# Decay attention and a top-128 expert layer in one kernel: the hand-written planner gets a limit of eight transfers under way, and new places for the operands of heads two and three

## The chip, the cores and the metric

The kernel runs on 1 core of one Trainium2 chip. The metric is device time in microseconds (us) from start to end of one execution; the time given for the kernel before is the median of 3 runs, 458.39 us (456.5 to 458.89). The engines are PE (matrix products and transposes), DVE (vector), ACT (activation), POOL (GpSimd) and SP, which here only issues transfers (DMAs). ACT issues a few DMAs too, at the start.

## The reference

Shapes: q, k, v are (8 batches, 8 heads, 576 rows, 64), f is (8, 8, 576). Everything is float32.

```python
scores = q @ k.T / sqrt(64)
cum = cumsum(log(clip(f, 1e-4, 1)), -1)
scores = where(causal, -1e9, scores + cum[:, None] - cum[None, :])
attn = softmax(scores);  o = attn @ v            # per batch and head
x = o with the heads side by side                # (8, 576, 512)
# per batch:
s = x @ w_gate;  top = the 128 rows with the largest s
h = relu(x[top] @ w1)                            # w1 is (512, 1024)
out = x;  out[top] += sigmoid(s[top]) * (h @ w2) # w2 is (1024, 512)
```

## The kernel before

**Heads and pairs.** The 64 heads are worked two by two, 32 pairs; the pairs of a batch are followed by the batch's expert layer, interleaved with the pairs of the next batch. Matrix products take float32 operands split into a rounded part and a rest. So a head `h` needs four operand tiles: `q2` (rounded q above, its rest below), `kk` (rounded k, twice), `qe` (rounded q and two rows of the decay) and `ke` (the rest of k and two rows of the decay). There are four sets of them, `q2_0` to `q2_3` and so on, used by head `h % 4`. `head_parts(h)` (L410) records what makes them:

- `t_load` (L419) loads q and k of the head into `raw` (two DMAs of 288 KB; three `raw` buffers),
- three casts `a0`, `a1`, `a2` (L448 to L451) make `q2`, `kk`, `qe`. Their line in the profile is L429 on ACT, L431 on DVE, L433 on POOL. For heads below `HELP1` = 16 any of the three engines may take them, later heads use POOL,
- two subtractions `a3`, `a4` (L456, L458; profile line L438) make the rests; DVE does them for heads 0 to 3, POOL for the others,
- the decay rows come by small DMAs: for heads 0 and 1 straight from `ep` in SBUF, issued by ACT (`ext`, profile line L463); for the others from DRAM copies `eq`, `eqr` (stored by ACT at L341, loaded by SP at L475, L478).

**A pair** (`pair_parts`, L492) has nine units, one per 128 rows of a head and one shared. In a unit PE makes scores `sc` (two products: L528 or L564 with `kk`, `q2`; L533 or L564 with `ke`, `qe`), DVE adds the mask and takes the row maximum `nm` (L538, L570, L576), ACT takes the exponential `p` (L589), PE transposes it into `tp` (L602, L620, L622), and ACT or DVE copies that to `pt` (L281, L283). When all nine are copied PE multiplies by v (`av`, L664), the result `ot` is copied and transposed back (`tb`, L717), and DVE normalises it and forms the gate's sums (L723 to L751). PSUM has eight banks, and scores, transposes and `av` all take from these eight.

**The expert layer** (`moe_parts`, L815): DVE counts for each row how many rows have a larger score (`rank`, L893, profile line L901; 14 operations per batch), then the chosen rows are gathered by POOL, transposed, multiplied by w1 and w2 on PE (L1017 to L1078), and scattered by POOL (L1089). The weights come in twelve parts (`weight_part`, L788).

**What sets the order.** Nothing is issued while it is recorded. Each step is handed to `Flow.add` (L58) with its cost in us on each engine that may do it, the steps it comes after, the buffers it takes and gives, and a `place`, a number that ranks it. `Flow.run` (L86) then plays the program on clocks of its own: for each engine it looks at the steps that can start within `EPS` of the earliest, picks the one with the smallest place, advances that engine's clock and issues the step. An engine's queue is in the order in which its steps were picked, and each engine executes its queue in that order. A transfer in the plan takes its time on SP's (or ACT's) clock to issue, 0.63 us for each DMA of a `load`, and its bytes at 240 KB/us on one bus (L113 to L116).

**Places.** `place` is counted in units, nine to a pair. `PS` (L184) sets how far ahead of its use a head's casts stand, `PL` (L183) its load, `PV` (L185) the load of v, `PM`, `PE_`, `PC` the maximum, exponential and copy of a unit, `WS`, `WD`, `WL` the weights, `RK`, `RD` the rank operations, `GO`, `GS`, `GL` the expert layer's products.

Of the kernel before, what the change touches and what calls it, by code (L numbers as in the profile page):

```python
# [30 lines left out]
class Flow:  # L31
# [7 lines left out]

    LAG = {"pe": 0.2, "act": 0.17, "dve": 0.12, "pool": 0.17, "sp": 0.05}  # L40
    OWN = {"pe": 0.0, "act": 0.1, "dve": 0.1, "pool": 0.08, "sp": 0.0}

# [4 lines left out]
    def __init__(self, slots, eps, bias, weight):  # L47
        self.free = {k: [0.0] * n for k, n in slots.items()}
        self.eps = eps
        self.bias = bias  # L50
        self.weight = weight
        self.kind = None
        self.clock = {}
        self.bus = 0.0
        self.ready = []
        self.todo = 0

    def add(self, cost, fn, after=(), place=0.0, take=(), give=(), lat=0.0, kind=None, dma=None):  # L58
        t = {"dma": dma, "cost": cost, "fn": fn, "place": place, "take": take, "give": give, "lat": lat, "kind": kind,
             "wait": 0, "next": [], "deps": [], "end": None, "eng": None, "n": self.todo}  # L60
        for d in after:
            if d is None:
                continue
            t["deps"].append(d)
            d["next"].append(t)
            t["wait"] += 1
        self.todo += 1
        if t["wait"] == 0:
            self.ready.append(t)
        return t  # L70

    def start(self, t, e):
# [4 lines left out]
        for k in t["take"]:  # L77
            n = need.get(k.name, 0)
            f = self.free[k.name]
            if len(f) <= n:  # L80
                return None
            s = max(s, f[n])
            need[k.name] = n + 1
        return max(s, self.clock.get(e, 0.0))

    def run(self, issued):  # L86
        left = self.todo
        while left:
# [24 lines left out]
            if t["dma"] is not None:  # L113

                self.bus = max(self.bus, self.clock[e] + 0.3) + t["dma"]
                t["end"] = self.bus + t["lat"]  # L116
            for k in t["give"]:
                k.end = max(k.end, t["end"] + self.LAG[e])
# [15 lines left out]
def kernel(  # L134
# [33 lines left out]
    BD = 0.35  # L168
    WP = 4
    WQ = 0  # L170
# [7 lines left out]
    LOOK = 6  # L178
    HELP1 = 16
    HELP2 = 4  # L180
    SPLIT = 2
    PR = -10.51
    PL = 19.99  # L183
    PS = 18.31  # L184
    PV = 9.46  # L185
    PM = 0.31
    PE_ = 0.16
    PC = -2.48
    PB = 1.68
    VO = -0.79  # L190
    VD = 1
    GD = 0.1
    WS = 56.75
    WD = 0.5
    WL = 7.32
    RK = 5.98
    RD = 5.85
    XP = 9.4
    GO = 21.21
    GS = 1.93  # L200
    GL = 4.48
    LG = 2.67
    SB = 3
# [87 lines left out]
    def load(fn, kb, n=1, slow=0.0, **kw):  # L291
        return add({"sp": 0.63 * n}, fn, lat=1.2 + slow, dma=kb / 240, **kw)

# [46 lines left out]
    def rows_store(dst, src, us, after, tk):  # L340
        return add({"act": 0.62}, lambda e: nc.scalar.dma_start(out=dst, in_=src().bitcast(F32)), lat=1.3 + us,  # L341
                   after=[after], place=PR, give=[tk])
# [67 lines left out]
    def head_parts(h):  # L410
# [34 lines left out]
        if h < HELP2:  # L445
            c2 = {"pool": 1.46, "dve": 0.9} if h > 3 else {"dve": 0.85}
        pl = base - PS
        a0 = add(c1, rounded(q2[:, cs], lambda: raws[h][:, 0, :]), after=both + old, place=pl)  # L448
# [12 lines left out]
        def ext(dst, src, after, tks, n=0.0):  # L461

            return add({"act": 0.62}, lambda e: nc.scalar.dma_start(out=dst.bitcast(F32), in_=src()), lat=1.3,  # L463
                       after=old + [after], place=h - 40 + n, give=tks)
# [27 lines left out]
    def pair_parts(p):  # L492
# [12 lines left out]

        lv = load(t_v, 288, 2, after=(ops[1][1][-1:] if p == 2 else []) + [d_rows] + avd[p - 3:p - 2] * (p > 2), place=9 * p - PV, take=[tk_v])

# [660 lines left out]
```

## Time and profile before

| | us |
|---|---|
| median of 3 runs | 458.39 |
| the profiled execution | 459.39 |
| its span, first to last instruction | 456.9 |
| PE busy | 430.4 (94% of the span) |
| DVE busy | 371.1 (81%) |
| ACT busy | 331.7 (73%) |
| POOL busy | 302.7 (66%) |

The span is what the rows below speak of; 2.5 us of the profiled execution lie around it. PE is busy for 94% of the span, so idle time of PE is what can be won or added. A row of the timeline gives the start, the duration, the engine, the line in the code, the operation with out<-in, and in brackets how long the engine had been idle before it and what released it. SPq and ACTq are rows of these engines' queues that issue DMAs: the time is that of the issue, not of the transfer.

### The profile page before, as it was taken

What the parts mean: (1) busy time and instruction counts of PE and PEld (TensorE: products, weight loads), DVE (VectorE), ACT (ScalarE), POOL (GpSimd) and SP (SyncE); (2) the same over time, 40 slices, a digit from 0 to 9 for tenths busy, and PEclk for the clock granted to TensorE, in tenths of its full rate; (3) what the DMA queues carried; (4) which work ended last, traced back from release to release, by engine and by line L of the source; (5) the groups of instructions that cost most, each with busy time, mean ns of one, the idle gap of its engine ahead of it and who ended that gap; (6) DMA issues with size and microseconds to landing.
All of it is one profiled execution on the core that took longest, in us unless ns stands there. A gap on an engine that the chain in (4) does not pass through costs nothing. (4 is left out here: it accounts for less than half of the span.)

```text
span 456.9 us, 10456 instructions
## 1 busy us (share of the span) xinstructions
PE 430.4 (94%) x3033; PEld 345.3 (76%) x3033; DVE 371.1 (81%) x1443; ACT 331.7 (73%) x999; POOL 302.7 (66%) x325
## 2 busy tenths in 40 slices
PE   1599999989999999999999999999999999999995
PEld 0588778866787878877877778887887778868773
DVE  7689889997899888999699868897698877885821
ACT  4599989987898787777787778877787678833220
POOL 6379989998899987767766858657667763011100
PEclk9999999998999999999999999999999999999998
DMA  7988869685669787796876586677686551022010
GB/s 189 222 233 231 218 168 248 177 238 156 186 167 241 190 222 188 183 226 165 221 184 180 131 215 160 151 197 182 180 216 159 142 164 45 0 77 76 23 46 24
DMA packets 50514, 75.64 MB, mean 166 GB/s; under 512 B 7863, under 2 KB 35546, under 8 KB 50458
## 3 DMA queue, kind: packets, MB, share of 16 engines
q1 hardware_dynamic: 48790, 70.19, 60.2%
q0 software_dynamic: 1280, 4.20, 2.8%
q10 hardware_dynamic: 388, 0.61, 0.5%
q8 instruction: 24, 0.39, 0.4%
q14 instruction: 32, 0.26, 0.2%
HBM read 56.75 MB, written 12.14 MB: 151 GB/s over the span
## 5 line engine op out<-in xcount | busy, mean ns | idle before, releaser
L589 ACT ACTIVATE p<-p,nm 128x512 f32<-128x512 f32 (+4 forms) x288 | 168.9, 592 | 26.2 <-DVE nm L538 24.3
L538 DVE CUSTOM_DVE_ANT_0 p<-sc,mask 128x384 f32<-128x384 f32 (+3 forms) x256 | 120.0, 484 | 26.9 <-PE sc L533 17.2
L281 ACT COPY pt<-tp 128x256 f32<-128x256 f32 (+3 forms) x246 | 98.5, 436 | 25.3 <-PE tp L602 21.7
L602 PE MATMUL tp<-ident,p 128*128 128x128 f32 x640 | 103.3, 281 | 6.0 <-ACT p L589 5.0
L528 PE MATMUL sc<-kk,q 128*128 128x384 f32 (+3 forms) x256 | 93.1, 368 | 12.5 <-DVE q L438 8.5
L438 POOL TENSOR_TENSOR q<-raw,q 64x576 fp32r<-64x576 f32 x60 | 85.9, 1432 | 12.0 <-DMA xe<-out_dram,idx 7.4
L664 PE MATMUL av<-pt,v 128*64 128x448 f32 (+4 forms) x768 | 93.7, 393 | 0.0
L602 PEld LDWEIGHTS tp<-ident,p 128*128 128x128 f32 x640 | 76.0, 143 | 20.1 <-ACT p L589 7.7
L438 POOL TENSOR_TENSOR ke<-raw,kk 64x576 fp32r<-64x576 f32 x60 | 86.3, 1439 | 4.1
L533 PE MATMUL sc<-ke,qe 68*128 68x384 f32 (+3 forms) x256 | 83.4, 337 | 1.8 <-DMA ke<-ep 1.8
L664 PEld LDWEIGHTS av<-pt,v 128*64 128x64 f32 x768 | 45.7, 137 | 43.5 <-issue 28.6
L433 POOL TENSOR_SCALAR q<-raw 128x576 fp32r<-128x576 f32 x57 | 38.8, 680 | 51.9 <-issue 19.5
L528 PEld LDWEIGHTS sc<-kk,q 128*128 128x128 f32 x256 | 50.2, 197 | 19.7 <-POOL mask L350 8.5
L589 ACT ACTIVATION_READ_ACCUMULATOR p<-p,nm 128x1 f32 x288 | 57.4, 199 | 0.0
L533 PEld LDWEIGHTS sc<-ke,qe 68*128 68x128 f32 x256 | 49.8, 196 | 3.7 <-ACT kk L429 2.2
L281 ACT COPY ot<-av 128x128 f32<-128x128 f32 x64 | 24.6, 398 | 25.7 <-PE av L664 25.5
L901 DVE TENSOR_SCALAR_CACHE_REDUCE j<-srow,sg 128x384 uint8<-128x384 f32 (+6 forms) x72 | 41.4, 575 | 1.2
L1089 POOL DMA_INDIRECT out_dram<-xe,idx x8 | 8.2, 1025 | 51.2 <-DVE xe L1085 49.0
L433 POOL TENSOR_SCALAR kk<-raw 128x576 fp32r<-128x576 f32 x56 | 38.5, 688 | 2.7 <-DMA raw<-in_qk_dram 2.7
L283 DVE COPY pt<-tp 128x128 f32<-128x128 f32 (+2 forms) x74 | 29.2, 401 | 4.6 <-PE tp L602 2.2
L564 PE MATMUL sc<-kk,q 128*128 128x288 f32 x128 | 30.0, 316 | 0.1
L564 PE MATMUL sc<-ke,qe 68*128 68x288 f32 x128 | 28.4, 305 | 0.0
(127 smaller groups left out, 756.8 us busy)
## 6 DMA issues: line engine op xcount, KB each, us to landing
raw<-in_qk_dram SPq DMA_DIRECT2D x128, 288.0 KB
v<-in_v_dram SPq DMA_DIRECT2D x32, 256.0 KB
out_dram<-x SPq DMA_DIRECT2D x16, 512.0 KB
qe<-q SPq DMA_DIRECT2D x41, 144.0 KB
srow<-sd SPq DMA_DIRECT2D x7, 320.0 KB
wst<-in_w_dram SPq DMA_DIRECT2D x4, 512.0 KB
wst<-in_w_dram SPq DMA_DIRECT2D x8, 256.0 KB
v<-in_v_dram SPq DMA_DIRECT2D x32, 32.0 KB
```

The source lines that it names most:

```text
L281: nc.scalar.copy(d, s_)
L283: nc.vector.tensor_copy(d, s_)
L433: nc.gpsimd.tensor_scalar(dst, src(), 1.0, 0.0, ALU.mult, ALU.add)
L438: (nc.vector if e == "dve" else nc.gpsimd).tensor_tensor(dst, a_(), b_, ALU.subtract)
L528: nc.tensor.matmul(st["sc", u][:, :n], q2s[r][:, q_slice(par, i)], kks[r][:, :n], start=True, stop=False)
L533: nc.tensor.matmul(st["sc", u][:, :n], qes[r][0:68, q_slice(par, i)], kes[r][0:68, :n], start=False, stop=True)
L538: nc.vector.tensor_tensor_reduce(out=st["p", u], in0=st["sc", u][:, :n], in1=mask[:, 512 - n:512], scale=-0.125, scalar=BIG, op0=ALU.add, ...
L564: nc.tensor.matmul(st["sc", u][g][:, :HALF], lt[0:kr, sl], rt[0:kr, g * HALF:(g + 1) * HALF], start=(n_ == 0 and m_ == 0), stop=(n_ == 1 a ...
L589: nc.scalar.activation(st["p", u], st["p", u], AF.Exp, bias=st["nm", u], scale=-1.0, accum_out=l)
L602: nc.tensor.transpose(tp[:, pos * P:(pos + 1) * P], st["p", u][:, j * P:(j + 1) * P], ident)
L664: nc.tensor.matmul(avb[g][par * D:(par + 1) * D, q0 - g * SPL:q1 - g * SPL], vt[:, j, par * D:(par + 1) * D], pt[:, off:off + q1 - q0], st ...
L901: nc.vector.tensor_scalar(junk[0:n, 0:w, :], src, sg()[0:n, c:c + 1], None, op, ALU.add, accum_out=cnt[0:n, k, c:c + 1])
```

## The change

`Flow` gets a list `lanes` with the planned end of every DMA in the order in which they are issued, and a constant of 8. A step that issues `k` DMAs can start no earlier than the end of the DMA that stands eight before its last. `load` passes its number of DMAs, the stores and `ext` on ACT pass 1. The casts and rests of heads 2 and 3 (counted from 0) get a place of their own, `P2` = 10 units ahead in place of `PS`. `HELP1` goes from 16 to 13, so casts of heads 13 to 15 are left to POOL; `WP` from 4 to 2, so only the first two weight parts may have their rest on DVE. The v of pair 1, like that of pair 2 before, is not loaded until the decay rows of head 1 are on their way. Twelve other numbers are set anew, most of them by a few hundredths to some tenths of a unit, `PS` from 18.31 to 12.18 and `PV` from 9.46 to 6.15. No operation is added or taken away; some change their engine.

```diff
+    LANES = 8
...
+        n = len(self.lanes) + t["k"] - 1 - self.LANES
+        if t["k"] and n >= 0:
+            s = max(s, self.lanes[n])
         return max(s, self.clock.get(e, 0.0))
...
+            self.lanes += [t["end"]] * t["k"]
...
-    WP = 4
+    WP = 2
...
-    HELP1 = 16
+    HELP1 = 13
     HELP2 = 4
+    P2 = 10
...
-    PS = 18.31
-    PV = 9.46
+    PS = 12.18
+    PV = 6.15
...
     def load(fn, kb, n=1, slow=0.0, **kw):
-        return add({"sp": 0.63 * n}, fn, lat=1.2 + slow, dma=kb / 240, **kw)
+        return add({"sp": 0.63 * n}, fn, lat=1.2 + slow, dma=kb / 240, k=n, **kw)
...
-        pl = base - PS
+        pl = base - (PS if h not in (2, 3) else P2)
...
-        lv = load(t_v, 288, 2, after=(ops[1][1][-1:] if p == 2 else []) + [d_rows] + avd[p - 3:p - 2] * (p > 2), place=9 * p - PV, take=[tk_v])
+        lv = load(t_v, 288, 2, after=(ops[1][1][-1:] if p in (1, 2) else []) + [d_rows] + avd[p - 3:p - 2] * (p > 2), place=9 * p - PV, take=[tk_v])
```

Lines of the new file are 8 higher from `head_parts` on. What the change does to the order shows at three places. The names in the rows carry the set or the unit: `kk_3` is `kk` of head 3, `raw3` its load, `p0_1` the exponential of pair 0, unit 1, `v1` the v of pair 1.

On SP, the queue of loads at the start; before:

```order
L422 DMA raw2_153<-in_qk_dram 64x1152 x2
L499 DMA v0_98<-in_v_dram 128x4x128
L502 DMA v0_98<-in_v_dram 64x128
L499 DMA v1_99<-in_v_dram 128x4x128
L502 DMA v1_99<-in_v_dram 64x128
L422 DMA raw3_196<-in_qk_dram 64x1152 x2
L499 DMA v2_100<-in_v_dram 128x4x128
L502 DMA v2_100<-in_v_dram 64x128
L422 DMA raw4_239<-in_qk_dram 64x1152 x2
```

and with the change:

```order
L430 DMA raw2_153<-in_qk_dram 64x1152 x2
L507 DMA v0_98<-in_v_dram 128x4x128
L510 DMA v0_98<-in_v_dram 64x128
L430 DMA raw3_207<-in_qk_dram 64x1152 x2
L430 DMA raw4_222<-in_qk_dram 64x1152 x2
L507 DMA v1_99<-in_v_dram 128x4x128
L510 DMA v1_99<-in_v_dram 64x128
```

Heads 3 and 4 are loaded ahead of v of pair 1; v of pair 2 has moved down behind the loads of heads 5 to 7.

On ACT, from the end of the `ext` DMAs to the first exponentials; before:

```order
L463 DMA ke_1_109<-ep_163 2x1x576
L429 CAST kk_1_108<-raw1_143 128x576
L429 CAST qe_1_107<-raw1_143 64x576
L341 DMA eq_78<-ep_163 64x1152
L341 DMA eqr_79<-ep_163 128x1x512
L341 DMA eqr_79<-ep_163 128x1x64
L429 CAST q2_2_110<-raw2_153 128x576
L429 CAST kk_2_112<-raw2_153 128x576
L429 CAST qe_2_111<-raw2_153 64x576
L589 ACTIVATE p0_0_180,st0_88<-p0_0_180,nm0_0_212 128x512
L429 CAST kk_3_116<-raw3_196 128x576
L429 CAST qe_3_115<-raw3_196 64x576
```

and with the change:

```order
L437 CAST kk_1_108<-raw1_143 128x576
L437 CAST qe_1_107<-raw1_143 64x576
L437 CAST q2_2_110<-raw2_153 128x576
L437 CAST kk_2_112<-raw2_153 128x576
L471 DMA ke_1_109<-ep_163 2x1x576
L349 DMA eq_78<-ep_163 64x1152
L349 DMA eqr_79<-ep_163 128x1x512
L349 DMA eqr_79<-ep_163 128x1x64
L597 ACTIVATE p0_0_178,st0_88<-p0_0_178,nm0_0_216 128x512
L597 ACTIVATE p0_1_185,st0_88<-p0_1_185,nm0_1_226 128x128
L597 ACTIVATE p0_2_188,st0_88<-p0_2_188,nm0_2_228 128x384
```

The casts of head 3 no longer stand between the first and the second exponential (POOL does them, and `qe_2`); the DMA of the decay rows of `ke_1` has moved behind the casts of head 2.

On DVE, about a fifth of the way through, the first rank operations (`j`); before:

```order
L746 TENSOR_REDUCE gu1_92<-tb5_1509 128x4x2
L901 TENSOR_SCALAR j0_0_1_1592,cnt_97<-srow0_1456,sg0_95 128x640
L901 TENSOR_SCALAR j0_1_0_1613,cnt_97<-srow0_1456,sg0_95 128x128
L901 TENSOR_SCALAR j0_1_1_1617,cnt_97<-srow0_1456,sg0_95 128x512
L901 TENSOR_SCALAR j0_2_0_1637,cnt_97<-srow0_1456,sg0_95 128x256
L901 TENSOR_SCALAR j0_2_1_1648,cnt_97<-srow0_1456,sg0_95 128x384
L751 TENSOR_REDUCE gu1_92<-tb45_1510 64x2
L901 TENSOR_SCALAR j0_3_0_1658,cnt_97<-srow0_1456,sg0_95 128x384
L538 ISA p8_0_1597,nm8_0_1670<-sc8_0_1596,mask_82 128x512
```

and with the change:

```order
L909 TENSOR_SCALAR j0_0_1_1547,cnt_97<-srow0_1419,sg0_95 128x640
L909 TENSOR_SCALAR j0_1_0_1551,cnt_97<-srow0_1419,sg0_95 128x128
L909 TENSOR_SCALAR j0_1_1_1558,cnt_97<-srow0_1419,sg0_95 128x512
L909 TENSOR_SCALAR j0_2_0_1564,cnt_97<-srow0_1419,sg0_95 128x256
L909 TENSOR_SCALAR j0_2_1_1569,cnt_97<-srow0_1419,sg0_95 128x384
L546 ISA p7_7_1519,nm7_7_1577<-sc7_7_1518,mask_82 128x384
L546 ISA nm7_7_1577 128x1
L738 TENSOR_TENSOR x1_0_1368<-tb45_1499,rn1_94 64x128
L746 TENSOR_TENSOR tb5_1498<-tb5_1498,wg_87 128x512
L291 COPY pt7_1427<-tq7_4_1592 128x2x64
L909 TENSOR_SCALAR j0_0_2_1605,cnt_97<-dg0_1553,sg0_95 128x128
L909 TENSOR_SCALAR j0_1_2_1612,cnt_97<-dg0_1553,sg0_95 128x128
```

The same five rank operations stand in one piece in both, but two units earlier with the change, ahead of the work on `tb5` and not near its end.

Over the whole program ACT has 10 casts of heads fewer, DVE 2, and POOL 12 more; ACT has 14 of the `pt` copies and 4 other small ones more, DVE as many fewer. From the middle of the program on, PE's queue is nearly the same in both.

## Rows read from the trace of the kernel before

**Rows 1.** The page's first line, and PE and DVE of its part 1 (busy us, share, instructions).

```profile
span 456.9 us, 10456 instructions
PE 430.4 (94%) x3033; PEld 345.3 (76%) x3033; DVE 371.1 (81%) x1443; ACT 331.7 (73%) x999; POOL 302.7 (66%) x325
```

**Rows 2.** The view of waits, of PE alone: who waited for whom; us in total, times, longest us.

```profile
PE sc L528 <- DVE q L438: 8.5, 1, 8.5
PE tp L602 <- ACT p L589: 5.0, 4, 3.9
PE sc L528 <- DVE nm L538: 2.5, 4, 1.4
PE sc L533 <- DMA ke<-ep: 1.8, 1, 1.8
PE sc L528 <- DVE gu L751: 1.3, 1, 1.3
```

**Rows 3.** Busy time of each engine in stretches of the span: stretch, its length, busy us of PE, of PE's weight loads, DVE, ACT, POOL (in brackets instructions), the granted clock of PE, the DMA engines' share, GB/s.

```profile
16.00:24.00 8.00, 3.75 (x18) 3.42 (x17) 4.89 (x12) 4.25 (x14) 0.68 (x2) 1.00 1.04 240
24.00:40.00 16.00, 16.00 (x112) 14.05 (x111) 14.30 (x52) 15.27 (x47) 14.41 (x13) 1.00 0.92 254
40.00:56.00 16.00, 16.00 (x130) 12.36 (x129) 14.69 (x56) 16.00 (x50) 15.16 (x14) 1.00 0.78 191
56.00:60.00 4.00, 2.72 (x19) 2.03 (x18) 2.27 (x9) 3.56 (x13) 3.08 (x3) 1.00 0.93 261
60.00:96.00 36.00, 35.84 (x286) 28.65 (x285) 33.40 (x119) 34.48 (x108) 34.54 (x33) 1.00 0.76 202
96.00:110.00 14.00, 11.77 (x76) 9.54 (x74) 13.42 (x58) 9.02 (x29) 13.69 (x15) 0.88 0.68 189
...
160.00:430.00 270.00, 269.93 (x1943) 216.65 (x1940) 227.05 (x921) 194.13 (x592) 162.63 (x164) 1.00 0.61 155
```

**Rows 4.** The timeline of PE in the first 25 us.

```profile
11.79 1.51 PE L533 MATMUL sc<-ke,qe 68*128 68x512 f32 x4 [1.80 <-DMA ke<-ep]
...
14.97 0.68 PE L564 MATMUL sc<-ke,qe 68*128 68x288 f32 x2
...
16.44 1.08 PE L602 MATMUL tp<-ident,p 128*128 128x128 f32 x4 [0.36 <-ACT p L589]
...
21.73 0.47 PE L602 MATMUL tp<-ident,p 128*128 128x128 f32 x1 [3.89 <-ACT p L589]
...
24.00 0.78 PE L528 MATMUL sc<-kk,q 128*128 128x512 f32 x1
```

**Rows 5.** The timeline of ACT in the same stretch.

```profile
8.53 0.59 ACTq L463 DMA_DIRECT2D ke<-ep  x1
...
10.96 0.67 ACT L429 CAST kk<-raw 128x576 fp32r<-128x576 f32 x1 [3.20 <-POOL q L399]
...
13.76 0.67 ACT L429 CAST q<-raw 128x576 fp32r<-128x576 f32 x1 [1.56 <-issue]
...
15.49 0.72 ACT L589 ACTIVATE p<-p,nm 128x512 f32<-128x512 f32 x1
...
20.04 0.67 ACT L429 CAST kk<-raw 128x576 fp32r<-128x576 f32 x1 [3.75 <-DMA raw<-in_qk_dram]
...
21.19 0.40 ACT L589 ACTIVATE p<-p,nm 128x128 f32<-128x128 f32 x1
```

**Rows 6.** The timeline of SP's queue, issues of DMAs: the load of f, the second part of v of pair 0, the load of head 3.

```profile
0.74 0.60 SPq L299 DMA_DIRECT2D fs<-in_f_dram  x1
...
11.48 0.47 SPq L502 DMA_DIRECT2D v<-in_v_dram  x1
...
13.79 1.30 SPq L422 DMA_DIRECT2D raw<-in_qk_dram  x2
```

**Rows 7.** Of SP's own waits the one of that second part of v (us in total, times, longest).

```profile
SPq L502 <- DMA qe<-ep: 1.9, 1, 1.9
```

**Rows 8.** The timeline of DVE: the first use of f.

```profile
3.38 0.45 DVE L302 TENSOR_SCALAR fs<-fs 64x576 f32<-64x576 f32 x1
```

**Rows 9.** Part 6 of the page, DMAs issued by POOL: the gather, with the median us from issue to landing at the end.

```profile
xe<-out_dram,idx POOLq DMA_INDIRECT x8, 4.8
```

**Rows 10.** Two stretches of 2 us behind the wait at 100 us; columns as in rows 3.

```profile
102.00:104.00 2.00, 2.00 (x11) 1.98 (x10) 2.00 (x13) 1.05 (x4) 2.00 (x3) 0.54 0.01 2
104.00:106.00 2.00, 2.00 (x13) 1.96 (x12) 2.00 (x9) 0.16 (x1) 2.00 (x3) 0.61 0.51 124
```

**Rows 11.** The timeline of DVE around 100 us: the first of five rank operations in a row, the sum behind them, the next maximum.

```profile
96.74 0.86 DVE L901 TENSOR_SCALAR_CACHE_REDUCE j<-srow,sg 128x640 uint8<-128x640 f32 x1
...
99.88 0.28 DVE L751 TENSOR_REDUCE gu<-tb 64x2 f32<-64x128 f32 x1
...
100.61 0.68 DVE L538 CUSTOM_DVE_ANT_0 p<-sc,mask 128x512 f32<-128x512 f32 x1
```

**Rows 12.** Of POOL's waits those for PE's use of an operand set (us in total, times, longest).

```profile
POOL q L433 <- PE sc L564: 15.7, 6, 4.0
```

**Rows 13.** The groups of instructions on POOL, shapes apart: the casts of `qe` (busy us, mean ns of one).

```profile
L433 POOL TENSOR_SCALAR qe<-raw 64x576 fp32r<-64x576 f32 x11 | 7.3, 667 | 0.0
```

**Rows 14.** The timeline of DVE: a cast while POOL only fills buffers, and one while POOL works on operands.

```profile
9.23 0.46 DVE L431 CAST q<-raw 128x576 fp32r<-128x576 f32 x1
...
33.47 1.54 DVE L431 CAST q<-raw 128x576 fp32r<-128x576 f32 x1
```

More of the change, by code (lines that the diff above doesn't have):

```diff
@@ L54, in __init__, with add @@
         self.bus = 0.0
+        self.lanes = []
         self.ready = []
         self.todo = 0
-    def add(self, cost, fn, after=(), place=0.0, take=(), give=(), lat=0.0, kind=None, dma=None):
-        t = {"dma": dma, "cost": cost, "fn": fn, "place": place, "take": take, "give": give, "lat": lat, "kind": kind,
+    def add(self, cost, fn, after=(), place=0.0, take=(), give=(), lat=0.0, kind=None, dma=None, k=0):
+        t = {"dma": dma, "k": k, "cost": cost, "fn": fn, "place": place, "take": take, "give": give, "lat": lat, "kind": kind,
              "wait": 0, "next": [], "deps": [], "end": None, "eng": None, "n": self.todo}
@@ L183 @@
     PL = 19.99
-    PS = 18.31
-    PV = 9.46
-    PM = 0.31
-    PE_ = 0.16
-    PC = -2.48
+    PS = 12.18
+    PV = 6.15
+    PM = 0.29
+    PE_ = 0.46
+    PC = -2.51
     PB = 1.68
-    VO = -0.79
+    VO = -0.72
     VD = 1
     GD = 0.1
[L193 to L196, printed above, removed]
+    WS = 57.83
+    WD = 0.54
+    WL = 7.27
+    RK = 6.1
     RD = 5.85
     XP = 9.4
-    GO = 21.21
+    GO = 20.64
     GS = 1.93
     GL = 4.48
-    LG = 2.67
+    LG = 2.5
     SB = 3
@@ L340, in rows_store @@
     def rows_store(dst, src, us, after, tk):
-        return add({"act": 0.62}, lambda e: nc.scalar.dma_start(out=dst, in_=src().bitcast(F32)), lat=1.3 + us,
+        return add({"act": 0.62}, lambda e: nc.scalar.dma_start(out=dst, in_=src().bitcast(F32)), lat=1.3 + us, k=1,
                    after=[after], place=PR, give=[tk])
@@ L461, in ext @@
         def ext(dst, src, after, tks, n=0.0):
-            return add({"act": 0.62}, lambda e: nc.scalar.dma_start(out=dst.bitcast(F32), in_=src()), lat=1.3,
+            return add({"act": 0.62}, lambda e: nc.scalar.dma_start(out=dst.bitcast(F32), in_=src()), lat=1.3, k=1,
                        after=old + [after], place=h - 40 + n, give=tks)
```

## The prediction

> **What bounds the kernel now.** I read the page's first part, then who PE waited for, then busy time by stretches, then the timelines where PE stood still. PE is busy for 430.4 of 456.9 us [rows 1], so 26.5 us are idle. From 160 to 430 us PE is busy for 269.93 of 270 us [rows 3]: there the work itself is the bound, and an order can only lose. What can be won lies before 160 us. PE's waits [rows 2] begin with 8.5 us ahead of its first product, on a chain of load, cast and rest that the change leaves alone. Next are 5.0 us for ACT's exponentials, 3.9 of them in one piece, at 21.73 us [rows 4]. The first stretch of rows 3 shows it as a hole: PE works 3.75 of 8 us, ACT 4.25, POOL 0.68, while the DMA engines are full.
>
> The cause stands on ACT [rows 5]. The exponential of unit 1 starts at 21.19, though its maximum was there long before; ahead of it in ACT's queue stand two casts of head 3, and the first starts at 20.04 after 3.75 us of waiting for that head's load. SP issued the load only at 13.79 [rows 6], behind v of pairs 0 and 1. Two smaller holes follow: 56 to 60 us, PE 2.72 of 4 us, where ACT comes from 16.00 busy of 16 us; and 96 to 110 us, PE 11.77 of 14 with the clock at 0.88 [rows 3]. In the second DVE runs five ranks in a row from 96.74, then the sum that frees a bank at 99.88 [rows 11], and PE waits 1.3 us for that sum [rows 2]. After it the granted clock is 0.54 and 0.61 for two stretches of 2 us [rows 10], so for most of 4 us it is at the lower of its two levels, 1.2 and not 2.4 GHz.
>
> **The change part by part.** All sums are against the profiled execution, 459.39 us (span 456.9 and 2.5 around it); it lies 1.0 above the median of the runs.
>
> *The start, gain.* On ACT the casts of head 3 leave the place between the first two exponentials. With the maxima done, unit 1's exponential follows unit 0's at once, and the wait of 3.89 at 21.73 [rows 4] goes. What is late next? POOL now casts head 3, after its load. The load is issued when two small DMAs of ACT have landed: the first of these held SP until 11.48 [rows 6, 7], so it goes out at about 11.5 in place of 13.79. Shifted by these 2.3 us alone it lands at 17.7 in place of 20.0; four casts at 0.67 [rows 13] and the two rests on DVE end near 22. PE first needs head 3 after all of pair 0's score work and the first half of pair 1's, past 24 us, so this is hidden by some 3 us. If POOL were 3 us later the gain would shrink from there on.
>
> *The start, loss.* The DMA of `ke_1`'s decay rows moves behind four casts of ACT. Before, these casts began at 10.96 and the third at 13.76, after the stores' issues [rows 5]; now the casts run through, and with four casts at 0.6 from 10.4 the DMA is issued at about 12.7 to 13.3. PE needs it for the second product of the shared unit, at 14.97 [rows 4]. How long such a DMA takes under this load: the like one of `ke_0`, issued from 8.53 to 9.12, let PE go on at 11.79 [rows 4, 5], 2.7 us after the issue. From below: the load of f, issued by 1.34, is used at 3.38, 2.0 us [rows 6, 8]. From above: 4.8 us, the gather's median [rows 9]. So it lands at 16.0 (15.3 to 18.1), and PE waits 1.0 us (0.4 to 3.1), of which 0.36 replaces the wait at 16.44 that stood there for the first exponential [rows 4]. I take 1.0, as that row is the same kind of transfer from the same queue.
>
> In the Trainium skill, page "DMA: Bandwidth & Descriptors", section "Queues, rings and completion order", each DMA engine takes turns between the queues that have work, packet by packet, so that ACT's small transfer would not stand behind the whole of SP's loads; by that rule the wait comes out near the lower end, 0.4 (the whole sum 453.7), and by a strict line behind head 3's 0.6 MB near the upper, 3.1 (456.4). The row of 2.7 us lies between.
>
> *Pair 0's `av`.* It now follows the last transpose of the pair with one product between, so PE waits for one copy, about 0.4 us.
>
> Start in all: 3.89 + 0.36 − 1.0 − 0.4 = 2.8 us gained (0.7 to 3.9).
>
> *ACT lighter.* From the first exponential to the fourth pair's `ot` copy the order has 7 casts of heads and one weight cast fewer on ACT, 7 × 0.6 + 1.0 = 5 us, against ten or so more copies at 0.3, so 2 us less; DVE has these copies less. The hole at 56 to 60 comes after 16 us of full ACT, and 2 us less is more than its 1.28. I count 1.3 gained (0 to 1.3).
>
> *POOL heavier.* 12 casts at 0.67 [rows 13] are 8.0 us, all in the first 16 heads. From 24 to 110 us POOL is busy for 80.9 of 86 us [rows 3], 5.1 idle; but from 16 to 24 it has 7.3 of 8 idle, which now holds work, as heads 3 and 4 come sooner. Also it waited 15.7 us for PE to give operand sets back [rows 12], which means it runs ahead. Cost 0 (0 to 8.0); the cover is that lead.
>
> *The ranks.* The five stand two units earlier, 3.2 us in one piece (96.74 to 99.88) [rows 11], now ahead of the work on `tb5`, which holds two of the eight banks; three more ranks come before its sums. PE has an `av` of pair 6 behind that block as cover. Before, the hole 96 to 110 cost 2.2 us of idle and about (1 − 0.54) × 2 + (1 − 0.61) × 2 = 1.7 us of lower clock [rows 3, 10]. I take it as unchanged: 0, with bounds of 3.9 won and 3.9 lost.
>
> *Everything else* (places by hundredths, the later half): PE's queue is nearly the same, and it has no idle time there: 0.
>
> Sum: 459.39 − 2.8 − 1.3 = 455.3, and with the median 1.0 lower 454.3 us.
>
> **The rivals.** *The later holes close too.* Every order is planned anew, and one that frees `tb5` in time wins the 3.9 us of the ranks: 450.4. For it: DVE is lighter. Against it: the five ranks still stand together.
>
> *The gain is given back.* `ke_1` lands at the upper end, the hole at 56 stays: 459.39 − 0.7 − 1.0 = 457.7, no change that can be told. The same comes out if the ranks' hole grows by 3.4. For it: the DMA engines are full at 16 to 24 [rows 3]. Against it: 2.7 us for `ke_0`.
>
> *POOL becomes the bound: slower.* The place is heads 5 to 15, the sign PE waiting for the rests on POOL in place of POOL waiting for PE. If POOL's lead is used up early, the 8.0 us come out on PE in full: 454.3 + 8.0 = 462.3. It is slower than before once more than 6.4 of the 8.0 are exposed. For it: 5.1 us idle are less than 8.0, and casts get longer beside one another: DVE's took 0.46 us while POOL only filled buffers and 1.54 us while POOL worked on operands [rows 14]. Against it: the lead of rows 12 and the free start.
>
> The Trainium skill, page "SBUF — State Buffer", section "Who interferes with whom", says that DVE and POOL share a pair of ports that one instruction holds to its end, and DVE's operations with two operands in SBUF or in a two-port mode take it. The two rows agree with it; by that rule each cast moved to POOL that meets one on DVE adds one of their lengths, which speaks for this rival. As the change takes 2 of DVE's 5 casts away it also meets less, and I leave its chance small.
>
> **How the numbers follow.** The forecast 454.3 has a chance of 0.44 (its own range 452 to 456), the closing of the later holes 0.2, the giving back 0.24, POOL 0.12. A measurement of this kernel can tell about 0.5%, 2.3 us: faster is below 456.1, slower above 460.7. Faster: nearly all of the first two and a quarter of the third, 0.43 + 0.2 + 0.06 = 0.69. Slower: three quarters of the last, 0.09. The same: 0.22. The range reaches from 450.0, the second case, to 459.0, beyond the third; what it leaves out is POOL and a part of the second.
>
> **What would show it.** PE's wait of 3.89 at ACT's exponential is gone, and the first product of pair 1 starts near 21 us where it was 24.00. PE waits for `ke` at about 15 us, by 0.4 to 3.1. ACT waits for no load of head 3. Between 56 and 60 us PE has no hole. From 160 us on the two traces run with one constant shift, equal to the gain. The forecast is wrong if that shift is there at 24 us and is smaller at 160; the waits of PE between say which rival it was. It is wrong in the other direction if the clock does not fall at 100 us.

## The result, and the profile after

With the change the kernel takes 460.75 us (median of 8 runs, 457.58 to 463.63); the kernel before, on the same chip, 458.17 us (8 runs, 456.20 to 459.46). The ratio is 1.0057 with a 95% interval of 1.0032 to 1.0083, so the change makes it slower by 0.6%, where 0.9% faster was forecast (454.3 against the 458.39 shown ahead of it). The profiled execution took 461.87 us. Its page begins, in answer to [rows 1]:

```profile
span 460.0 us, 10416 instructions
PE 434.2 (94%) x3033; PEld 347.1 (75%) x3033; DVE 365.1 (79%) x1423; ACT 328.9 (71%) x1007; POOL 309.9 (67%) x337
```

PE's idle time has shrunk a little, 25.8 us against 26.5, and PE is busy 3.8 us longer for the same instructions. The waits and stretches tell where. PE's waits [rows 2] are now:

```profile
PE sc L536 <- DVE q L446: 8.6, 1, 8.6
PE sc L541 <- DMA ke<-ep: 2.1, 1, 2.1
PE tp L610 <- DVE nm L546: 1.7, 1, 1.7
PE sc L536 <- POOL q L446: 1.3, 1, 1.3
...
PE sc L541 <- POOL ke L446: 1.1, 2, 1.0
```

The 3.9 us behind ACT's exponential are gone, and PE waits for POOL, which it never did to speak of before. Where it happens shows in the stretches [rows 3] (columns as there):

```profile
16.00:24.00 8.00, 8.00 (x42) 7.48 (x41) 6.97 (x19) 6.24 (x21) 5.18 (x7) 1.00 0.86 237
24.00:40.00 16.00, 15.50 (x113) 12.46 (x114) 13.29 (x52) 14.06 (x47) 13.54 (x14) 1.00 0.78 183
40.00:56.00 16.00, 13.89 (x114) 10.69 (x110) 13.85 (x47) 14.45 (x43) 15.46 (x14) 1.00 0.93 224
56.00:60.00 4.00, 3.73 (x16) 3.54 (x17) 1.34 (x6) 2.26 (x8) 3.83 (x5) 0.57 0.69 207
60.00:96.00 36.00, 35.83 (x283) 28.12 (x282) 32.23 (x118) 31.78 (x100) 30.77 (x32) 1.00 0.77 199
96.00:110.00 14.00, 12.22 (x78) 8.84 (x79) 13.58 (x57) 11.67 (x37) 12.68 (x13) 1.00 0.70 202
110.00:130.00 20.00, 17.33 (x129) 13.75 (x127) 12.92 (x63) 15.93 (x50) 16.62 (x17) 0.91 0.72 200
130.00:160.00 30.00, 29.77 (x208) 24.29 (x205) 26.29 (x102) 21.68 (x69) 28.00 (x29) 1.00 0.67 172
160.00:230.00 70.00, 68.56 (x511) 53.81 (x510) 57.10 (x245) 56.86 (x182) 58.00 (x58) 1.00 0.80 201
230.00:430.00 200.00, 199.90 (x1425) 160.67 (x1424) 165.28 (x659) 140.04 (x432) 111.26 (x113) 1.00 0.56 146
```

and the kernel before in the three stretches that [rows 3] lack:

```profile
110.00:130.00 20.00, 19.32 (x154) 14.88 (x153) 14.89 (x70) 18.02 (x59) 16.43 (x18) 1.00 0.67 187
130.00:160.00 30.00, 28.57 (x205) 22.88 (x205) 27.77 (x105) 24.16 (x78) 28.73 (x28) 1.00 0.80 195
160.00:230.00 70.00, 69.93 (x526) 56.53 (x523) 60.59 (x252) 54.95 (x174) 53.53 (x54) 1.00 0.80 203
```

Read as idle time plus the time lost to the clock (length times one minus the granted clock), after less before: 16 to 24 us −4.25; 24 to 56 us +2.6; 56 to 60 us −1.0 idle and +1.7 clock; 96 to 110 us −0.45 idle and −1.7 clock; 110 to 130 us +2.0 idle and +1.8 clock; 130 to 160 us −1.2; 160 to 230 us +1.4. The start is won in full. How much of it is left shows in DVE's maxima of equal number, by their starts in both traces: with the change they come 4.1 us earlier at 45 us, 0.5 at 78, 0.2 at 110, and 3 to 4 us later nearly everywhere from 230 to the end.

This list does not add up to the 3.1 us by which the span grew: with the two ends of the span it comes out near 0, because PE is also busy longer where its granted clock is full. The starts of PE's products do add up. Taking the time from each product to the next, less the median for its kind in both traces, after less before gives −4.5 us up to 30 us, +3.2 from 30 to 60, −0.8 from 60 to 110, +4.0 from 110 to 130, −1.7 from 130 to 160 and +2.9 from 160 to 230. So there are three places of loss: 45 to 60, 110 to 130, and 160 to 230 us, where the orders differ and the lag of the maxima hides it.

The start itself, in answer to [rows 4 to 6], on PE, ACT and SP's queue:

```profile
12.20 1.51 PE L541 MATMUL sc<-ke,qe 68*128 68x512 f32 x4 [2.08 <-DMA ke<-ep]
...
19.91 0.78 PE L536 MATMUL sc<-kk,q 128*128 128x512 f32 x1
```

```profile
11.77 0.57 ACTq L471 DMA_DIRECT2D ke<-ep  x1
...
15.31 0.38 ACT L597 ACTIVATE p<-p,nm 128x128 f32<-128x128 f32 x1
```

```profile
11.48 3.00 SPq L430 DMA_DIRECT2D raw<-in_qk_dram  x4
```

The first product of pair 1 starts at 19.91 and not at 24.00. The load of head 3 is issued at 11.48. The late decay rows of `ke_1` cost PE nothing in this profile: it takes them up at 15.38 us without a wait, 3.6 us after their issue.

The loss at 120 us, first on POOL (the gather, the cast of `qe`, the q rest and the `ke` rest of head 20):

```profile
116.62 1.17 POOL L962 DMA_INDIRECT xe<-out_dram,idx  x1 [0.18 <-DVE pt L291]
117.84 0.68 POOL L441 TENSOR_SCALAR qe<-raw 64x576 fp32r<-64x576 f32 x1
121.45 1.40 POOL L446 TENSOR_TENSOR q<-raw,q 64x576 fp32r<-64x576 f32 x1 [2.93 <-DMA xe<-out_dram,idx]
122.92 1.39 POOL L446 TENSOR_TENSOR ke<-raw,kk 64x576 fp32r<-64x576 f32 x1
```

then on PE, in its timeline:

```profile
122.90 0.50 PE L536 MATMUL sc<-kk,q 128*128 128x512 f32 x1 [1.33 <-POOL q L446]
124.37 0.66 PE L541 MATMUL sc<-ke,qe 68*128 68x512 f32 x1 [0.97 <-POOL ke L446]
```

and the stretch behind these waits, columns as in [rows 3]:

```profile
125.00:128.00 3.00, 3.00 (x16) 2.78 (x15) 1.82 (x9) 2.11 (x7) 3.00 (x5) 0.51 0.80 199
```

POOL issues the gather of batch 0, casts `qe` of head 20, and then stands for 2.93 us before that head's q rest, until the gather has landed. The rest has nothing to do with the gathered rows. PE waits for it and for the `ke` rest, 2.3 us, and in the 3 us from 125 on the granted clock is 0.51, nearly all at the lower level of 1.2 GHz.

POOL's own waits (us in total, times, longest) tell that this is no single case. Of the kernel before:

```profile
POOL q L438 <- DMA xe<-out_dram,idx: 7.4, 5, 2.4
```

and with the change:

```profile
POOL q L446 <- DMA xe<-out_dram,idx: 15.8, 6, 4.6
...
POOL q L446 <- DMA out_dram<-xe,idx: 10.9, 4, 3.3
```

Each time the first q rest behind an indirect transfer, gather or scatter, waits for its landing: 7.4 us before, 26.7 with the change. POOL's instruction list, with the semaphores on which each waits, says why; the changed kernel around the first gather:

```
128 L962 DMA xe0_0_1934<-out_0_dram,idx0_0_1918 128x512 [waits DVE_49]
129 L441 TENSOR_SCALAR qe_0_103<-raw20_1560 64x576 [waits PE_49]
130 L446 TENSOR_TENSOR q2_0_102<-raw20_1560,q2_0_102 64x576 [waits DMASW0_49,Pool_49]
131 L446 TENSOR_TENSOR ke_0_105<-raw20_1560,kk_0_104 64x576
```

`DMASW0` is the gather's semaphore. Of POOL's steps the first q rest behind each of these ten transfers carries such a wait, in both programs (it is the first behind the transfer that also waits for a result of POOL itself; why the wait is put there is not shown). Before, that rest is the seventh row behind the first gather, and the gather has landed when POOL gets there:

```profile
120.36 1.17 POOL L954 DMA_INDIRECT xe<-out_dram,idx  x1 [1.17 <-DVE rn L694]
...
126.33 1.42 POOL L438 TENSOR_TENSOR q<-raw,q 64x576 fp32r<-64x576 f32 x1
```

Now it is the second. So the order decides whether the landing costs anything, and the planner knows nothing of it.

### The profile page after: what moved, and what is told of

It is laid out like the page before. It is cut to its first block, busy times and chain, and to the rows that moved or that the text cites. A ratio compares the mean times of both kernels' runs of the same rounds, so it can differ in the third digit from the quotient of the medians.

```text
span 460.0 us, 10416 instructions
## 1 busy us (share of the span) xinstructions
PE 434.2 (94%) x3033; PEld 347.1 (75%) x3033; DVE 365.1 (79%) x1423; ACT 328.9 (71%) x1007; POOL 309.9 (67%) x337
## 5 line engine op out<-in xcount | busy, mean ns | idle before, releaser
L597 ACT ACTIVATE p<-p,nm 128x128 f32<-128x128 f32 (+4 forms) x288 | 168.8, 590 | 30.1 <-DVE nm L546 26.0
L546 DVE CUSTOM_DVE_ANT_0 p<-sc,mask 128x512 f32<-128x512 f32 (+3 forms) x256 | 119.9, 485 | 34.7 <-PE sc L541 22.8
L289 ACT COPY pt<-tp 128x256 f32<-128x256 f32 (+3 forms) x256 | 101.4, 425 | 25.2 <-PE tp L610 20.6
L610 PE MATMUL tp<-ident,p 128*128 128x128 f32 x640 | 105.1, 281 | 3.8 <-DVE nm L546 1.7
L536 PE MATMUL sc<-kk,q 128*128 128x512 f32 (+3 forms) x256 | 93.8, 369 | 12.3 <-DVE q L446 8.6
L541 PE MATMUL sc<-ke,qe 68*128 68x512 f32 (+3 forms) x256 | 84.0, 340 | 3.2 <-DMA ke<-ep 2.1
L441 POOL TENSOR_SCALAR kk<-raw 128x576 fp32r<-128x576 f32 x60 | 41.4, 689 | 2.9 <-DMA raw<-in_qk_dram 2.8
L291 DVE COPY pt<-tp 128x128 f32<-128x128 f32 (+3 forms) x64 | 27.5, 433 | 8.5 <-PE tp L610 4.5
```

The lines of the kernel that those rows point to most:

```text
L289: nc.scalar.copy(d, s_)
L291: nc.vector.tensor_copy(d, s_)
L441: nc.gpsimd.tensor_scalar(dst, src(), 1.0, 0.0, ALU.mult, ALU.add)
L536: nc.tensor.matmul(st["sc", u][:, :n], q2s[r][:, q_slice(par, i)], kks[r][:, :n], start=True, stop=False)
L541: nc.tensor.matmul(st["sc", u][:, :n], qes[r][0:68, q_slice(par, i)], kes[r][0:68, :n], start=False, stop=True)
L546: nc.vector.tensor_tensor_reduce(out=st["p", u], in0=st["sc", u][:, :n], in1=mask[:, 512 - n:512], scale=-0.125, scalar=BIG, op0=ALU.add, ...
```

## Experiments

In all but three kernels the order is held: `Flow.run` plans as it did, and what it planned is changed at a few steps, then issued.

```diff
-            t["fn"](e)
-            issued()
+            plan.append([t, e])
+        for t, e in edited(plan):
+            t["fn"](e)
+            issued()
```

Steps are named by the number in which they are recorded. "Before" below is the kernel before, run with each set on the same chip (457.4 to 457.9 us).

### The indirect transfers behind the q rests

Nine of the ten are moved just behind the q rest ahead of which they stand (the tenth stands behind one already), then the first alone, then the first two:

```diff
+    for n, m in [(2693, 851), (2771, 1255), (2741, 1499), (2819, 1831), (2927, 1911), (2897, 2155), (3005, 2235), (2975, 2479), (3083, 2559)]:
+        x = plan.pop(at(n))
+        plan.insert(at(m) + 1, x)
```

```diff
+    for n, m in [(2693, 851)]:
```

```diff
+    for n, m in [(2693, 851), (2771, 1255)]:
```

> The changed kernel with its order held fixed on every engine but for nine indirect transfers of POOL: each now stands one or more rows later, behind the next head's q rest instead of ahead of it. Theory 1 (a q rest that follows an indirect transfer on POOL waits until that transfer has landed, and PE waits for POOL at 122.9 and 124.4 us for that reason): the 2.93 us POOL wait at 121.45 is gone, PE's waits of 1.33 and 0.97 us and the 3.4 us at half clock behind them (1.7 us) go with it, so about 4 us by 134 us, and part of the 2.5 us that are lost between 177 and 223 us, where the same wait is 4.63 us: 455 to 457.5 us in all, near or under the kernel before. Rival A (POOL has too much work since it got 12 casts more, and the wait for the transfer only takes up time that POOL would lose elsewhere): PE still waits for POOL's rests near 123 us, gain under 1.5 us, 459.5 to 461. Rival B (the PE time is lost to the granted clock, whatever the waits): the second half-clock stretch comes back elsewhere, gain about 2 us, 458.5.

> The changed kernel with one step moved: the gather of batch 0 stands behind the q rest of the head it stood ahead of. Theory 1 (of the ten q rests that wait for an indirect transfer only those count for which PE has no spare head; the first is the costliest, since PE's waits of 1.33 and 0.97 us and a half-clock stretch hang on it): 456 to 457.5 us, some 4 of the 6.6 us that all nine moves gave. Rival (the gain of the nine moves is spread over all transfers, as the POOL waits are: 2.9 us here of 26.7 in all): 460 us.

> The changed kernel with the gathers of batches 0 and 1 moved behind the q rests, the eight later transfers left as they are. Theory 1 (after 230 us the changed kernel and the kernel before run at a constant distance although POOL waits 17 us more there, so the later waits are covered by POOL's spare time): the same as all nine moves, 454 to 454.8 us. Rival (the later waits count too): 456 to 458.

Measured: nine moves 454.15 us, ratio to before 0.9927 (0.9903 to 0.9950); the first alone 455.48, 0.9960 (0.9924 to 0.9997); two 454.73, 0.9942 (0.9917 to 0.9968). Against the changed kernel's 1.0057 one moved instruction is worth 1.0%, 4.4 us, and nine 1.3%, 6 us. Theory 1 stands in all three, though nine moves and the first alone came out 0.9 and 0.5 us better than its ranges. With the first alone, POOL's timeline reads:

```profile
113.21 0.67 POOL L441 TENSOR_SCALAR qe<-raw 64x576 fp32r<-64x576 f32 x1
113.96 1.42 POOL L446 TENSOR_TENSOR q<-raw,q 64x576 fp32r<-64x576 f32 x1
115.67 1.17 POOL L962 DMA_INDIRECT xe<-out_dram,idx  x1 [0.30 <-POOL q L446]
116.91 1.40 POOL L446 TENSOR_TENSOR ke<-raw,kk 64x576 fp32r<-64x576 f32 x1
```

and the stretch in which the clock fell with the change:

```profile
122.00:126.00 4.00, 4.00 (x36) 2.38 (x34) 3.17 (x8) 1.74 (x6) 3.84 (x5) 1.00 0.71 194
```

POOL does the same work, with all 12 casts, PE has no wait here (4.00 busy of 4.00 us) and its clock is full: the amount of POOL's work was not the cause. In this run POOL still waits 24.0 us for eight later landings (13.1 and 10.9), and all of that costs some 0.33%, the difference to the nine moves, which the overlapping intervals don't tell from nothing. The loss at 160 to 230 us is still there:

```profile
160.00:230.00 70.00, 68.58 (x512) 53.98 (x511) 57.45 (x233) 56.34 (x179) 57.94 (x59) 1.00 0.79 199
```

The second gather's move takes back 0.2 of these 1.4 us of idle time, and nine moves no more (68.76 us busy); what is left are PE's waits of 0.2 to 0.6 us for copies of ACT and a result of DVE, whose cause was not tested.

### The rests on DVE

The gather stays in its place, and the two rests behind it leave POOL:

```diff
+    for n, e in {850: 'dve', 851: 'dve'}.items():
+        plan[at(n)][1] = e
```

> The changed kernel with its order held fixed, and the gather of batch 0 where the change puts it; only the q and ke rests of the head behind it go from POOL to DVE, at the same place of the plan. Theory 1 (POOL stops at the first rest behind a gather because that rest carries a wait for the landing, and PE waits for that rest): the wait moves to the next q rest on POOL, seven rows later, where the gather has landed; PE's waits of 1.33 and 0.97 us for POOL go, DVE pays for two rests of about 0.9 us each among its maxima: 457 to 459.5 us. Rival (PE would have waited there for another reason): 460 to 462.

Measured: 455.25 us, ratio 0.9950 (0.9932 to 0.9968), better than expected. The rests on DVE took 0.76 and 0.74 us, not 0.9. The wait for the landing moved to the next head's q rest, where nothing is left of it:

```profile
113.67 1.17 POOL L962 DMA_INDIRECT xe<-out_dram,idx  x1 [0.18 <-DVE pt L291]
...
122.80 1.41 POOL L446 TENSOR_TENSOR q<-raw,q 64x576 fp32r<-64x576 f32 x1
```

### The planner told of the landing

A rule in the planner, and a new plan, which is the old one up to just behind the first gather:

```diff
+        if e == "pool" and t["kind"] == "rest":
+            s = max(s, self.land)
...
+            if t["kind"] == "indirect":
+                self.land = t["end"] + self.LAG[e]
```

The rests are marked "rest", gather and scatter "indirect", and the gather's planned time to land goes from 3.2 to 3.6 us. Then the same without the limit of eight transfers (`LANES = 100000`), and the rule alone on the kernel before.

> The changed kernel with one rule more in the planner: a rest on POOL starts no earlier than the landing of the last indirect transfer that POOL issued; the order is planned anew with it, and is the same up to the first gather. The plan then puts five casts behind the first gather ahead of a rest. Theory 1 (this wait was the cause, and the planner avoids it once it is told): no wait of POOL's rests for a landing over 1.5 us, no wait of PE for POOL near 120 us, 453.5 to 455.5 us. Rival (any new order of the later part scatters by several us, whatever the rule): 456 to 460.

> The planner with the landing rule, the change's constants and own places, but without the limit of eight transfers under way. Theory 1 (at the start the limit keeps the small transfers and weights behind the heads' loads, and most of the 4 us come from the constants and own places anyway): PE 2 to 4 us earlier than before at 40 us, 453 to 456 us. Rival (the limit is what makes the plan fit the chip): no lead at 40 us, 457 or more.

> The kernel before with the landing rule alone in its planner; its order is the same up to 164 us. Theory 1 (before, POOL's waits for landings, 7.4 us in five, stand where POOL has time to spare, so the rule gives nothing): 456.5 to 458.5 us, no change. Rival (the rule is a gain of its own, and the 452.5 us of the planner that was told owe half to it): 454 to 455.5.

Measured: 452.53 us, ratio 0.9902 (0.9872 to 0.9931), the fastest of all; without the limit 454.09, 0.9918 (0.9901 to 0.9934); the rule on the kernel before 457.55, 1.0002 (0.9983 to 1.0021). So the rule gives nothing where no wait was exposed, and the plan that it makes turns the change from 0.6% slower to 1.0% faster. With it PE's busy time in the later stretches is:

```profile
110.00:130.00 20.00, 19.62 (x146) 14.51 (x144) 16.77 (x67) 16.37 (x51) 19.48 (x20) 1.00 0.71 193
160.00:230.00 70.00, 69.86 (x536) 56.68 (x537) 60.88 (x251) 57.80 (x185) 59.37 (x59) 1.00 0.83 214
230.00:430.00 200.00, 199.90 (x1403) 161.13 (x1402) 165.32 (x664) 136.71 (x419) 108.40 (x109) 1.00 0.54 140
```

One part of the expectation missed: POOL's rests still wait up to 4.0 us for a landing in the later half, where it costs PE nothing. Of the 26.7 us of such waits 21.1 are left, so the gain is not the absence of waits. Against the run with the first gather moved, whose maxima come at the same times up to 114 us, this one is 3.4 us shorter in the profile, and the idle time at 160 to 230 us has gone from 1.4 to 0.14: that part of the gain is the new order there, and the runs don't separate the rule from it. The limit of eight transfers is not what the gain hangs on: without it the start is worth about 2 us in place of 4, and the time is 1.6 us longer, with intervals that overlap.

### The start alone

The kernel before, with only the loads and casts of the start moved as the change has them:

```diff
+    for n, e in {120: 'pool', 121: 'pool', 113: 'pool'}.items():
+        plan[at(n)][1] = e
+    for n, m in [(198, 118), (126, 198), (214, 213), (120, 119), (121, 120), (113, 17)]:
+        x = plan.pop(at(n))
+        plan.insert(at(m) + 1, x)
```

> The kernel before with its order held fixed but for the start: the loads of heads 3 and 4 go out ahead of pair 1's v, pair 2's v goes later, and three casts of heads 2 and 3 go from ACT to POOL. This is the step of the prediction that was worth 2.8 us. Theory 1 (a lead won at the start is carried through, as nothing else in the order changes): PE is 3 to 4 us earlier at 40 us and 2 to 4 us at the end, 454 to 456 us. Rival (PE is not what bounds 50 to 64 us: there POOL is busy 97 per cent and DVE holds the banks, so a PE that comes earlier only waits longer): 3 us ahead at 40 us, under 1 us at 64 us, 457 to 458.5.

Measured: 456.50 us, ratio 0.9958 (0.9939 to 0.9977), 1.9 us, between the two theories. It is not the mechanism of either: PE waited 2.4 us up to 21.8 for a maximum, ahead of which DVE, still in the order made for the late head 3, ran that head's two rests, then PE ran 6.8 us at half clock; 0.7 us of lead was left at 40 us. From 108 us on the lead is 2.2 to 2.3: the other 1.5 came at the ranks, where in this run the clock did not fall. So the start needs the other queues' new order too, and this run doesn't test whether a lead is carried. The run with the first gather moved comes nearer to that: its span is 3.5 us shorter than before, with other gains and losses between.

### The weight rest at 52 us

The loss at 52 to 60 us begins with PE's 1.72 us for a maximum; ahead of it DVE runs the rest of the first weight part, and it is long. PE, DVE and POOL, changed kernel, then DVE and POOL of the run with the first gather moved:

```profile
54.87 0.30 PE L610 MATMUL tp<-ident,p 128*128 128x128 f32 x1 [1.72 <-DVE nm L546]
...
56.27 0.58 PE L536 MATMUL sc<-kk,q 128*128 128x256 f32 x1 [0.66 <-DVE nm L546]
```

```profile
51.80 2.31 DVE L816 TENSOR_TENSOR w1l<-wst,w1h 128x1024 fp32r<-128x1024 f32 x1
```

```profile
51.62 1.42 POOL L446 TENSOR_TENSOR q<-raw,q 64x576 fp32r<-64x576 f32 x1
53.11 2.27 POOL L446 TENSOR_TENSOR ke<-raw,kk 64x576 fp32r<-64x576 f32 x1
```

```profile
51.34 1.17 DVE L816 TENSOR_TENSOR w1l<-wst,w1h 128x1024 fp32r<-128x1024 f32 x1
```

```profile
51.48 2.31 POOL L446 TENSOR_TENSOR q<-raw,q 64x576 fp32r<-64x576 f32 x1
53.86 1.39 POOL L446 TENSOR_TENSOR ke<-raw,kk 64x576 fp32r<-64x576 f32 x1
```

The same two instructions in the same order: where DVE starts 0.14 us ahead it takes 1.17 and POOL's rest 2.31; where POOL starts 0.18 us ahead it takes 1.42 and DVE's 2.31. PE's wait follows: 1.72, 1.01, 0.93, 0.65, 0.57 and 0.58 us in six profiles with this order, each 0.6 less than the weight rest's 2.31, 1.60, 1.53, 1.25, 1.17 and 1.17. Only after the longest did the clock fall at 57 us. I tried to mend it: cut in quarters behind the next maxima, and moved whole to 63 us, each on the changed kernel and with the nine moves.

```diff
+    for n, (w, ms) in {2630: (1024, (385, 390, 395, 408))}.items():
+        t, e = plan.pop(at(n))
+        for k, m in enumerate(ms):
+            c = slice(k * w // len(ms), (k + 1) * w // len(ms))
+            p = dict(t, n=n if k + 1 == len(ms) else n + 0.1 * (k + 1), fn=lambda e, t=t, c=c: t["fn"](e, c))
+            plan.insert(at(m) + 1, [p, e])
```

```diff
+    for n, m in [(2630, 277)]:
```

> The changed kernel with its order held fixed but for the first rest of the expert weights on DVE (the 2.31 us one at 51.8 us): it is cut into four quarters that stand behind the second, third, fourth and fifth of the unit maxima that follow. Theory 1 (this one instruction, stretched from an estimated 1.7 by the port that it shares with POOL, holds up the maxima, PE waits 1.72 and 0.66 us for them and then runs 3.4 us at half clock): PE's waits at 54.9 and 56.3 us and the half-clock stretch at 57 go, PE is 3 to 4 us earlier at 60 us; at the end 457 us if it carries through, since nothing mends the loss at 123 us. Rival A (DVE is simply full there: the quarters hold up the next maxima instead): PE waits as long in 55 to 62 us, gain under 1 us. Rival B (the lead is gained at 60 us but given back at the ranks or where POOL waits at 121 us): 3 us ahead at 60 us, under 1 us at 140 us, 460 to 461 in all.

> Both edits together, otherwise the changed kernel's order. If the two causes are right and independent, the gains add: 461 - 4 - 3.5 - part of 2.5 = 452 to 454 us, which is under the kernel before by about 1 per cent, and the lead of 4 us that the start gives is still there at the end. Rival (the two stretches share one limit, so that closing one opens the other): no better than the better of the two alone, 456 to 458.

> All nine indirect transfers behind the q rests, and the first rest of the expert weights on DVE moved whole from 51.8 us to the end of the gate's work at about 63 us, where PE had no wait in the run with two gathers moved. Theory 1 (the weight rest and POOL's rests use one port in turn: whichever starts first holds it to its end, so 0.2 us decides whether the weight rest takes 1.17 or 2.31 us, and ahead of unit maxima that costs PE up to 1.2 us and half clock behind it): PE's wait near 53 us falls to about 0.5 us in every run, 453 to 454 us and a smaller spread than the 453.2 to 457.5 of the nine moves alone. Rival (moved later it holds up other maxima): 455 to 456.

> The changed kernel with only the weight rest moved to about 63 us, the indirect transfers left where the change puts them. Theory 1 (both causes are real and separate, the gathers worth 5 to 6 us and the weight rest the rest): 457.5 to 459.5 us, and PE still waits for POOL's q and ke rests at about 120 us. Rival A (what the lead is lost by at 52 to 60 us is given back anyway by the wait at 120): 460 to 461.5. Rival B (the weight rest is the greater cause): under 457.

Measured: quarters alone 463.15 us, 1.0128 (1.0096 to 1.0161), with the nine moves 457.43, 0.9992 (0.9971 to 1.0014); later alone 462.04, 1.0105 (1.0073 to 1.0138), with the nine moves 456.31, 0.9974 (0.9952 to 0.9996). Each is by 0.5 to 0.7% slower than the same kernel with the weight rest in place (in three of these four pairs the intervals lie apart; for later alone they overlap), so my theory of the remedy fell; the rivals by which the pieces, or the later place, hold up other maxima come nearest. The quarters point to one reason:

```profile
53.15 0.97 DVE L816 TENSOR_TENSOR w1l<-wst,w1h 128x256 fp32r<-128x256 f32 x1
54.52 0.41 DVE L816 TENSOR_TENSOR w1l<-wst,w1h 128x256 fp32r<-128x256 f32 x1
```

Of the four quarters one takes 0.41 us, with hardly any work of POOL beside it, and three take 0.85 to 0.97 beside POOL; that four meet POOL more often than one is argued from this, and no run tests it alone. Moved to 63 us, the wait at 53 does fall to 0.43, as expected, but PE then waits 0.77 us at 54.6, where it waited 0.66, and 0.73 us at 55.8, which is new. Why PE's third wait comes in when the weight rest is gone was not settled.

## Why the prediction was wrong

**The start was right and undersized.** Forecast 2.8 us (0.7 to 3.9); PE's first product of pair 1 came 4.1 us earlier, though PE's work on `ke_0` began 0.4 us later (12.20 and not 11.79). The load of head 3 went out at 11.48, as worked out. Two terms were charged that did not come in the profile of the changed kernel: the 1.0 for `ke_1`, whose DMA was issued at 11.77 and not at 12.7 to 13.3, and the 0.4 for pair 0's copy. That was luck in part: of the ten profiles with this order at the start the wait for `ke_1` came in one (0.83 us, with nine transfers moved), and a wait for a DVE copy ahead of pair 0's `av` in seven (0.24 to 0.69 us, and once 1.77).

**The hole at 56 to 60** was to close, for 1.3. It moved forward: 24 to 60 us has 2.9 us idle after and 1.3 before. With the first gather moved, 40 to 60 us still has 1.2 us idle. This term was 0, and in the profile of the changed kernel less than 0, by the weight rest and the clock.

**The ranks** were to be unchanged within 3.9 either way. Idle time was (0.45 us less), but the clock did not fall there as it had in [rows 10], 1.7 us less lost; at 110 us the lag of the maxima shows little of it. That is the sign that the forecast named for an error in the other direction, and it was there.

**"POOL heavier ... Cost 0 (0 to 8.0); the cover is that lead"** is the step that failed. Its casts cost nothing that shows: with one gather moved and all of them on POOL, PE waits 0.2 us for POOL in the whole span. But the step counted POOL's work and not its order: behind the first gather POOL's lead goes in one piece, 2.93 us, and 2.3 us of waits and 1.8 us of clock come out on PE; moving that gather alone gave back 4.4 us of the 6.4 by which the forecast missed. The rival of slower had the right sign, PE waiting for POOL's rests, at heads 5 to 15; it came at head 20 and from another cause, and the casts that it priced were not it. The row that held the term was in the view of POOL's waits of the kernel before, 7.4 us in five for landings of gathers; the forecast took from that view only the 15.7 us of [rows 12].

**"Everything else: 0"** failed too: between 160 and 230 us there is 1.4 us of new idle time, and by the starts of PE's products 2.9 us are lost. A further landing stops POOL there for 4.6 us, but moving that gather too gained 0.2%, which the intervals do not tell from nothing. With the planner's new order the loss is gone; its cause stays open.

Without these waits the change is worth nearly what was forecast: with nine transfers moved 0.7% (454.15 us) where 0.9% was forecast (454.3). Part of that agreement is chance, since the start gave more and the hole less. Outside this sum the profile of the changed kernel lost some 3 us at 52 to 60 us, against the run with the first gather moved, to DVE's long weight rest and the clock; its runs spread over 6 us, which fits, though no run separates that share.

## What to carry to other kernels

Where an engine issues transfers and also computes, look in its own waits for a computation that waits for a transfer it doesn't use, and count the instructions from each transfer to the first that carries the wait: an order that shortens that distance can cost more than the change that made it wins. A planner should know such waits; with one rule here its plan was 1.5% faster, 1.0% of which a single moved transfer gives too. And a wait costs only what the engine behind it has not in reserve: nearly the same order had 24 us of such waits for almost nothing and one of 2.93 us for 1%. Last, check that the places of loss add up to the loss: idle time and granted clock alone showed less than half of the 2.9 us lost at 160 to 230 us here.

## What the runs showed of the hardware

- A subtraction on DVE and one on POOL, both on operands in SBUF, ran one after the other and not side by side: 1.17 and 2.31 us, or 2.31 and 1.42, by a start 0.14 to 0.18 us apart. The Trainium skill, page "SBUF — State Buffer", section "Who interferes with whom", says that one instruction holds the shared pair of ports to its end; these rows agree, and they add that the same two instructions in the same order came out differently from profile to profile.
- PE's waits of 1.72 and 0.66 us at 54.9 and 56.3 us were followed by 3.4 us at half clock (0.57 in 56 to 60 us), those of 1.33 and 0.97 us by as much, a loss of 1.7 us each. In the three profiles with the first gather's wait mended and the weight rest in its place (one gather, two, the rests on DVE) the clock did not fall behind either; with nine transfers moved it fell once before the end, at 27.0 us, behind a wait of 1.77 us at 25.6. At these three places a stall of some 2 us cost nearly twice itself. What decides it is not shown: with the quarters it fell at 56.7 us behind waits of 0.43, 0.74 and 0.62 us, and with the weight rest moved whole it did not fall there behind 0.43, 0.77 and 0.73. Nor does the granted clock tell all: at 14 us in the changed kernel two products of 288 columns take 0.68 us, as they do at a granted clock of 0.50 in the run of the start alone (25.85 us), and at 28 us 0.43, while 1.00 is on record for both.
- A gather of 128 rows landed 3.3 to 6.2 us after its issue by POOL in the profile of the changed kernel, and 3.2 to 7.3 us over all profiles. How many instructions cover it is not fixed: in the kernel before, the wait was gone at the seventh instruction behind the first gather, and at the fourth behind the other five it was 0.6 to 2.4 us.
